# LSH attention and two MLP layers: products with v of the second batch four steps behind the scores, and the second layer's first w_in products ahead of the first layer's last w_out products

## Chip, cores and metric

One core of a Trainium2 chip. The metric is the device time of one execution in microseconds; the time before is a median of three runs. Engines: TensorE (PE; PEld is its weight load), VectorE (DVE), ScalarE (ACT), GpSimd (POOL), SyncE (SP, which here only issues transfers).

## What is computed

Attention in which a query sees only the keys of its own bucket (the signs of six projections), and then two MLP layers on the result, with sigmoid gates.

```python
# q, k, v: (2, 8, 768, 64); proj: (64, 6); w_in: (512, 2048); w_out: (2048, 512), two layers
mask = q_bucket[:, :, :, None] == k_bucket[:, :, None, :]
scores = np.where(mask, scale * np.matmul(q, k.transpose(0, 1, 3, 2)), -1000000000.0)
attn = np.exp(scores - np.max(scores, axis=-1, keepdims=True))
attn = attn / (np.sum(attn, axis=-1, keepdims=True) + 1e-09)
attn_out = np.matmul(attn, v)
x = attn_out.transpose(0, 2, 1, 3).reshape(B * S, H * D)      # 1536 x 512
h = x @ w_in;  g = h * (1.0 / (1.0 + np.exp(-1.702 * h)));  x = g @ w_out
h = x @ w_in2; g = h * (1.0 / (1.0 + np.exp(-h)));          return g @ w_out2
```

## The kernel before

**Precision.** Large operands are kept as a high and a low part, so that each layer product is three matmuls (`three` in `gemm2`, the inner loop of `gemm1`), and a product with v takes three per key block.

**Attention.** The 16 heads have six steps each, 96 steps in all; a step is 128 queries against 768 keys. `scores` (L408) makes four matmuls into the tile `pss`. `top` (L422) takes the row minimum on VectorE and copies the scores to `p`; `exps` and `p_high` run on ScalarE, `p_low` (L443) on GpSimd writes the low half into `hl`. Two steps share one `hl`: `p_turn` (L447) turns both on the odd step by one transposing transfer from SP's queue into `pt` (two buffers). `av` (L454) multiplies `pt` with v, 18 matmuls a step into `pav`, `norm` divides and turns the result into the MLP's tokens `XH`, `XL`. `ahead` prepares the next pair of heads on all engines; its `rows` (L355) copies bucket rows by four transfers on SP.

**Two batches.** The loop at L583 runs steps 0 to 47 and then 48 to 95. `LAG = 3` says how many steps later `av(j)` is written than the score step j's own turn. In the second batch `scores` has one buffer of `pss`, and between the steps the loop yields to the generator `mlp` of the first layer for token blocks 0 and 1 (`RATE` layer units a step).

**Layers.** `mlp` (L615) works in units of one to four slices of d_ff. For each unit and token block `gemm1` makes `psh` = x w_in and the gate (ScalarE L640, VectorE L641, ScalarE's cast to `gh` L642, GpSimd's `gl` L643), and `gemm2` makes `pso` = g w_out and adds it up in `part` (VectorE L675). `gemm2` of a unit and block is written behind `gemm1` of the next one; the last is written alone (L690). After the attention follow the first layer on blocks 2 and 3 (L762) and the second layer on all four (L765). Weights come as 64-bit words: `Weights.step` loads one piece (`raw`), makes fp32 of it by five operations (L173 ScalarE, L174 to L178 VectorE), then a high part (L180 ScalarE) and a low one (L181 GpSimd). One step is taken at each yield (`background`, L716).

**Order.** A scheduler sorts the instructions by priority into one queue for each engine, and each engine works its queue in order. `sooner` raises a task's priority by the offsets of `SOONER`: in the second batch `av` stands highest among the attention's tasks (400), `scores` has 200.

```python
            for i in range(first - lead, last + LAG + 1):
...
                at(av, i - LAG)
                at(top, i + lead - 1)
...
                at(p_turn, i - TUL)
                yield i
                if lead == 1:
                    at(scores, i + 1)
```

Of the kernel before, what the change touches and what calls it, by code (L numbers as in the profile page):

```python
# [21 lines left out]
def tile_lsh_attention_two_mlps(  # L22
# [15 lines left out]
    B, H, S, D = q.shape  # L38
# [23 lines left out]
    NBUF = 3  # L62
    LAG = 3
    TUL = 1
# [16 lines left out]
    RATE = (3.4, 2.85)  # L81
    SWITCH = HEADS // 2 * NC + LAG + 1
    RING = 3
# [168 lines left out]
    def attention(sp, s1, ps_m, ps_v, ahead_of, setup):  # L252
# [155 lines left out]
        def scores(j):  # L408
            n, c = steps[j]
            aq, ak = st["q", n], st["k", n]  # L410
            bq, bk = BQ[place(n)], BK[place(n)]
            ps = ahead_of["pool"].tile([P, 2, 512], F32, tag="s", name="pss")
            lq = aq.rearrange("p a b -> p (a b)")[:, c * P:(c + 1) * P]
            bq = bq[:, c * P:(c + 1) * P]
            for half in range(2):
                o = ps[:, half, 0:HS]
                T.matmul(o, lhsT=lq, rhs=ak[:, half, :], start=True, stop=False)  # L417
                T.matmul(o, lhsT=bq, rhs=bk[:, half * HS:(half + 1) * HS], start=False, stop=True)  # L418
            st["S", j] = ps[:, :, 0:HS]
# [34 lines left out]
        def av(j):  # L454
# [5 lines left out]
            o = st["av", g][:, c * (D + 1):(c + 1) * (D + 1)]  # L460
            for i in range(NC):
                hv, lv = vs[:, n % 2, i, 0:D + 1], vs[:, n % 2, i, D + 1:]
                T.matmul(o, lhsT=pt[:, i], rhs=hv, start=(i == 0), stop=False)  # L463
                T.matmul(o[:, 0:D], lhsT=pt[:, i], rhs=lv, start=False, stop=False)  # L464
                T.matmul(o, lhsT=pt[:, NC + i], rhs=hv, start=False, stop=(i == NC - 1))  # L465

# [115 lines left out]

        for lead, first, last in ((2, 0, N // 2), (1, N // 2, N)):  # L583
            def at(f, j):
# [30 lines left out]
    def mlp(layer, blocks, units, W, mp, ps_h, tanh, keep=()):  # L615
# [70 lines left out]
        for i, u in enumerate(seq):  # L686
            yield from gemm1(*u)
            if i != 1:
                yield from gemm2(*seq[max(i - 1, 0)])
        yield from gemm2(*seq[-1])  # L690

# [69 lines left out]
    ps_h = ctx.enter_context(tc.tile_pool(name="ps_h", bufs=8, space=PSUM))  # L761
    for _ in mlp(0, [2, 3], [first1] + cut, W, mp, ps_h, False):  # L762
        background()
    base = NF + len(again)
    for _ in mlp(1, [0, 1, 2, 3], [list(range(f, f + 4)) for f in range(base, base + NF, 4)], W, mp, ps_h, False):  # L765
        background()
# [30 lines left out]
```

## Time and profile before

| | |
|---|---|
| median of 3 runs | 806.49 us (803.45 to 806.79) |
| profiled execution, its own time | 809.91 us |
| its span | 807.9 us |
| PE busy | 740.4 us (92%) |
| DVE, ACT, POOL busy | 507.3, 422.4, 430.4 us |
| chain that ended last, by engine | PE 66%, DMA 13%, DVE 10%, issue 4%, ACT 3%, POOL 2% |

A busy PE counts modelled ends of pipelined matmuls. The first batch of the attention fills the span up to about 157 us, the second batch with the first layer's blocks 0 and 1 up to 394, the first layer's blocks 2 and 3 up to 530, and the second layer the rest.

### The profile page before, as it was taken

Reading aid. Unit: us, or ns where it says so; the run is one execution under the profiler, and the core shown is the slowest. Engines: PE = TensorE matmul, PEld = TensorE weight load, DVE = VectorE, ACT = ScalarE, POOL = GpSimd, SP = SyncE. Lnnn points to the kernel's source line nnn. Section 1 sums busy time; section 2 is a strip of 40 time slices with the busy share of each in tenths; the row PEclk is TensorE's granted clock in tenths of the full one; section 3 lists DMA queues with packets and bytes.
Section 4 is the critical chain, followed back from the end, with each engine's and each line's share of the span. In section 5 each row is a group of like instructions: output and inputs, shape, how many; then the busy total and the mean of one; then the engine's idle time right before and its main releaser. Section 6 shows DMA issues by size and latency. Waiting matters only on the chain.

```text
span 807.9 us, 14034 instructions
## 1 busy us (share of the span) xinstructions
PE 740.4 (92%) x5384; PEld 682.6 (84%) x5384; DVE 507.3 (63%) x932; ACT 422.4 (52%) x721; POOL 430.4 (53%) x345
## 2 busy tenths in 40 slices
PE   6786777678889999899999999979999999999998
PEld 5676666668878898899899999978998899989996
DVE  8987688967689798887332244999545744322222
ACT  6776576586778586676444134445545333311220
POOL 5675567877659666766633133567535334422220
PEclk9898888799999999999999999999999999999999
DMA  5999999999999998885597040333211300000112
GB/s 160 206 191 186 185 204 208 211 247 249 272 225 252 255 227 239 220 188 106 149 387 246 2 157 1 130 108 101 80 52 53 105 1 2 0 1 1 40 40 78
DMA packets 196270, 116.40 MB, mean 144 GB/s; under 512 B 153318, under 2 KB 175846, under 8 KB 196204
## 3 DMA queue, kind: packets, MB, share of 16 engines
q1 hardware_dynamic: 196044, 115.52, 57.5%
q8 instruction: 42, 0.69, 0.3%
q14 instruction: 24, 0.20, 0.1%
q10 hardware_dynamic: 160, 0.00, 0.0%
HBM read 56.63 MB, written 16.78 MB: 91 GB/s over the span
## 4 chain that ended last, share of the span: by engine, by line
PE 66%; DMA 13%; DVE 10%; issue 4%; ACT 3%; POOL 2%; SPq 0%; ACTq 0%; DVEq 0%; POOLq 0%
PE pso L666 29%; PE psh L632 28%; DMA pt<-hl 9%; PE pss L417 2%; PE psbit L345 2%; POOL hl L445 2%; DMA raw<-in_moe_w_in_dram 2%; DVE p L425 2%; PE pss L418 2%; DVE f L176 1%; ACT p L430 1%; PE pav L463 1%; PE pav L464 1%; PE pav L465 1%; DVE f L175 1%
## 5 line engine op out<-in xcount | busy, mean ns | idle before, releaser
L643 POOL TENSOR_TENSOR gl<-g,gh 128x384 fp32r<-128x384 f32 x128 | 136.0, 1064 | 195.7 <-ACT gh L642 183.6
L445 POOL TENSOR_TENSOR hl<-p,hl 128x768 f16<-128x768 f32 x96 | 162.6, 1700 | 71.9 <-ACT hl L441 37.4
L632 PE MATMUL psh<-XH,wih 128*128 128x384 f32 x512 | 174.2, 340 | 1.5 <-DVE part L675 1.0
L632 PE MATMUL psh<-XL,wih 128*128 128x384 f32 x512 | 172.9, 338 | 1.8 <-DVE XL L498 1.8
L632 PE MATMUL psh<-XH,wil 128*128 128x384 f32 x512 | 173.2, 338 | 0.0
L675 DVE SCALAR_TENSOR_TENSOR part<-pso,part 128x384 f32<-128x384 f32 (+1 forms) x124 | 72.6, 591 | 88.8 <-PE pso L666 88.6
L641 DVE TENSOR_TENSOR g<-g,psh 128x384 f32<-128x384 f32 x96 | 52.8, 551 | 117.5 <-ACT g L640 117.5
L430 ACT ACTIVATE p<-p,lo 128x768 f32<-128x768 f32 x96 | 89.7, 936 | 52.7 <-DVE p L425 52.2
L642 ACT CAST gh<-g 128x384 fp32r<-128x384 f32 x128 | 65.5, 513 | 78.7 <-DVE g L641 69.1
L425 DVE TENSOR_SCALAR_CACHE_REDUCE p<-pss 128x768 f32<-128x768 f32 x96 | 90.8, 948 | 15.3 <-PE pss L418 13.3
L632 PEld LDWEIGHTS psh<-XH,wih 128*128 128x128 f32 x512 | 97.5, 190 | 3.1 <-ACT XH L677 1.0
L632 PEld LDWEIGHTS psh<-XL,wih 128*128 128x128 f32 x512 | 97.6, 191 | 2.8 <-DVE XL L498 2.2
L632 PEld LDWEIGHTS psh<-XH,wil 128*128 128x128 f32 x512 | 97.3, 190 | 0.2 <-POOL wil L181 0.2
L640 ACT ACTIVATE g<-psh 128x384 f32<-128x384 f32 x96 | 46.8, 489 | 96.1 <-PE psh L632 95.2
L463 PE MATMUL pav<-VS,pt 128*128 128x65 f16 x576 | 64.4, 198 | 33.9 <-DMA pt<-hl 32.1
L666 PE MATMUL pso<-gh,woh 128*128 128x384 f32 x256 | 87.3, 347 | 6.5 <-ACT gh L642 4.3
L463 PEld LDWEIGHTS <-pt 128*128 128x128 f16 x576 | 54.6, 99 | 44.1 <-DMA pt<-hl 38.9
L666 PE MATMUL pso<-gh,wol 128*128 128x384 f32 x256 | 86.2, 337 | 0.0
L666 PE MATMUL pso<-gl,woh 128*128 128x384 f32 x256 | 86.1, 336 | 0.0
L417 PE MATMUL pss<-ak,aq 128*128 128x384 f32 x192 | 76.0, 397 | 10.8 <-DVE p L425 10.5
L666 PE MATMUL pso<-woh,gh 128*128 128x512 f32 x192 | 74.8, 390 | 0.2 <-ACT gh L642 0.2
L666 PE MATMUL pso<-wol,gh 128*128 128x512 f32 x192 | 75.0, 391 | 0.0
(119 smaller groups left out, 1572.0 us busy)
## 6 DMA issues: line engine op xcount, KB each, us to landing
raw<-in_moe_w_in_dram SPq DMA_DIRECT2D x32, 512.0 KB
raw<-in_moe_w_out_dram SPq DMA_DIRECT2D x32, 512.0 KB
spih<-wih SPq DMA_DIRECT2D x13, 256.0 KB
spil<-wil SPq DMA_DIRECT2D x13, 256.0 KB
spoh<-woh SPq DMA_DIRECT2D x13, 256.0 KB
spol<-wol SPq DMA_DIRECT2D x13, 256.0 KB
wih<-spih SPq DMA_DIRECT2D x13, 256.0 KB
wil<-spil SPq DMA_DIRECT2D x13, 256.0 KB
```

The lines of the kernel that those rows point to most:

```text
L417: T.matmul(o, lhsT=lq, rhs=ak[:, half, :], start=True, stop=False)
L425: V.tensor_scalar(p, st.pop(("S", j)), LOW, None, op0=ALU.min, op1=ALU.min, accum_out=lo)
L430: A.activation(p, p, AF.Exp, bias=lo, scale=-1.0)
L445: G.tensor_tensor(out=hl[:, 1], in0=st.pop(("p", j))[0], in1=hl[:, 0], op=ALU.subtract)
L463: T.matmul(o, lhsT=pt[:, i], rhs=hv, start=(i == 0), stop=False)
L632: T.matmul(h, lhsT=a[:, c], rhs=x[t][:, c], start=(n == 0), stop=(n == 3 * NDC - 1))
L640: A.activation(g, h, AF.Sigmoid, scale=beta)
L641: V.tensor_tensor(out=g, in0=g, in1=h, op=ALU.mult)
L642: A.copy(gh[:, f], g)
L643: G.tensor_tensor(out=gl[:, f], in0=g, in1=gh[:, f].bitcast(F32), op=ALU.subtract)
L666: T.matmul(y, lhsT=a, rhs=x, start=(n == 0), stop=(n == 3 * nf - 1))
L675: V.scalar_tensor_tensor(out=acc, in0=y, scalar=scale, in1=acc, op0=ALU.mult, op1=ALU.add)
```

## The change

`LAG` becomes a pair: three steps in the first batch, four in the second. In the second batch the products of step j are also tied behind the last score matmul of step j + 4 on TensorE (`issue_after`), so that the scheduler can't put them sooner; the last four steps, which have no such matmul, are free. `mlp` yields once more, "last", ahead of its last `gemm2`; at this place in the first layer's blocks 2 and 3 the caller takes four units of the second layer, its `gemm1` of the first four slices on block 0, each with a step of the weights.

```diff
-    LAG = 3
+    LAGS = (3, 4)
...
-    SWITCH = HEADS // 2 * NC + LAG + 1
+    SWITCH = HEADS // 2 * NC + LAGS[0] + 1
...
-                T.matmul(o, lhsT=bq, rhs=bk[:, half * HS:(half + 1) * HS], start=False, stop=True)
+                st["did", j] = T.matmul(o, lhsT=bq, rhs=bk[:, half * HS:(half + 1) * HS], start=False, stop=True).ins
...
-            for i in range(NC):
-                hv, lv = vs[:, n % 2, i, 0:D + 1], vs[:, n % 2, i, D + 1:]
-                T.matmul(o, lhsT=pt[:, i], rhs=hv, start=(i == 0), stop=False)
-                T.matmul(o[:, 0:D], lhsT=pt[:, i], rhs=lv, start=False, stop=False)
-                T.matmul(o, lhsT=pt[:, NC + i], rhs=hv, start=False, stop=(i == NC - 1))
+
+            first = st.get(("did", j + 4)) if j >= N // 2 else None
+            with tc.issue_after(first) if first is not None else nullcontext():
+                for i in range(NC):
+                    hv, lv = vs[:, n % 2, i, 0:D + 1], vs[:, n % 2, i, D + 1:]
+                    T.matmul(o, lhsT=pt[:, i], rhs=hv, start=(i == 0), stop=False)
+                    T.matmul(o[:, 0:D], lhsT=pt[:, i], rhs=lv, start=False, stop=False)
+                    T.matmul(o, lhsT=pt[:, NC + i], rhs=hv, start=False, stop=(i == NC - 1))
...
-        for lead, first, last in ((2, 0, N // 2), (1, N // 2, N)):
+        for lead, first, last, LAG in ((2, 0, N // 2, LAGS[0]), (1, N // 2, N, LAGS[1])):
...
                 yield from gemm2(*seq[max(i - 1, 0)])
+        yield "last"
         yield from gemm2(*seq[-1])
...
-    for _ in mlp(0, [2, 3], [first1] + cut, W, mp, ps_h, False):
+    base = NF + len(again)
+    second = mlp(1, [0, 1, 2, 3], [list(range(f, f + 4)) for f in range(base, base + NF, 4)], W, mp, ps_h, False)
+    for at_end in mlp(0, [2, 3], [first1] + cut, W, mp, ps_h, False):
         background()
-    base = NF + len(again)
-    for _ in mlp(1, [0, 1, 2, 3], [list(range(f, f + 4)) for f in range(base, base + NF, 4)], W, mp, ps_h, False):
+
+        if at_end == "last":
+            for _ in range(4):
+                next(second)
+                background()
+    for _ in second:
         background()
```

In the changed kernel the lines from `scores` on have numbers one to four higher. How it moves instructions, first in the second batch on TensorE, around the first product of step 78 (before: `pt_5266`, after the scores of step 81, `pss_5268`):

```order
L666 MATMUL pso_4004<-gh_3750,wol_3698 128x384
L417 MATMUL pss_5268<-ak_4192,aq_4271 128x384
L418 MATMUL pss_5268<-BK2_160,BQ2_156 128x384
...
L463 LDWEIGHTS pt_5266
L463 MATMUL pav_5273<-VS0_170,pt_5266 128x65
```

Now (`pt_5243` is steps 78 and 79, `pss_5245` and `pss_5286` are the scores of steps 81 and 82):

```order
L418 MATMUL pss_5245<-ak_4174,aq_4253 128x384
L419 MATMUL pss_5245<-BK2_160,BQ2_156 128x384
...
L467 MATMUL pav_5042<-VS0_170,pt_5157 128x65
...
L418 MATMUL pss_5286<-ak_4174,aq_4253 128x384
L419 MATMUL pss_5286<-BK2_160,BQ2_156 128x384
...
L636 MATMUL psh_3769<-XH1_64,wih_3492 128x384
...
L467 LDWEIGHTS pt_5243
L467 MATMUL pav_5291<-VS0_170,pt_5243 128x65
```

The products of step 78 stood right behind the scores of step 81. Now step 77's (`pt_5157`) stand there, and step 78's come behind the scores of step 82 and a unit of w_in.

On SP, the transfers between the transpositions of pairs 66 and 68 before (L186 stores parts of weights, L360 copies bucket rows):

```order
L451 DMA_TRANSPOSE pt_4465<-hl_4280 128x24x128
L186 DMA spih7_3148<-wih_3137 128x512
L292 DMA nv_4659<-in_v_dram 128x2x384
L360 DMA BK1_159<-mk_4448 13x768
L186 DMA spil7_3150<-wil_3138 128x512
L360 DMA BQ1_155<-mk_4448 13x768
L139 DMA raw_3411<-in_moe_w_out_dram 128x512
L360 DMA BK2_160<-mk_4448 13x768
L360 DMA BQ2_156<-mk_4448 13x768
L451 DMA_TRANSPOSE pt_4668<-hl_4462 128x24x128
```

Now those between pairs 68 and 70:

```order
L452 DMA_TRANSPOSE pt_4650<-hl_4439 128x24x128
L187 DMA spol6_3107<-wol_3095 128x512
L187 DMA spih7_3130<-wih_3119 128x512
L140 DMA raw_3355<-in_moe_w_in_dram 128x4x128
L361 DMA BK1_159<-mk_4425 13x768
L187 DMA spil7_3132<-wil_3120 128x512
L361 DMA BQ1_155<-mk_4425 13x768
L361 DMA BK2_160<-mk_4425 13x768
L361 DMA BQ2_156<-mk_4425 13x768
L452 DMA_TRANSPOSE pt_4825<-hl_4647 128x24x128
```

The four copies of bucket rows moved from ahead of pair 68's transposition to ahead of pair 70's; the next four stand ahead of pair 82's now, which before stood ahead of pair 78's.

At the change of layers, VectorE before (`g_7315` and `g_7333` are the third and fourth gate of the second layer's first unit, `f_...` are pieces of weights in conversion):

```order
L174 TENSOR_SCALAR f_7192<-f_7192 128x512
L175 TENSOR_SCALAR f_7192<-f_7192 128x512
L176 SCALAR_TENSOR_TENSOR f_7192<-raw_7131,f_7192 128x512
L641 TENSOR_TENSOR g_7315<-g_7315,psh_7302 128x384
L178 SCALAR_TENSOR_TENSOR f_7192<-raw_7131,f_7192 128x512
L174 TENSOR_SCALAR f_7211<-f_7211 128x512
L175 TENSOR_SCALAR f_7211<-f_7211 128x512
L176 SCALAR_TENSOR_TENSOR f_7211<-raw_7150,f_7211 128x512
L641 TENSOR_TENSOR g_7333<-g_7333,psh_7320 128x384
```

Now (`g_7275` and `g_7293` are the third and fourth gate, `part_6150` to `part_6186` the first layer's last sums):

```order
L175 TENSOR_SCALAR f_7192<-f_7192 128x512
L679 SCALAR_TENSOR_TENSOR part_6150<-pso_7298,part_6150 128x384
L176 TENSOR_SCALAR f_7192<-f_7192 128x512
L679 SCALAR_TENSOR_TENSOR part_6162<-pso_7305,part_6162 128x384
L645 TENSOR_TENSOR g_7275<-g_7275,psh_7262 128x384
L679 SCALAR_TENSOR_TENSOR part_6174<-pso_7312,part_6174 128x384
L177 SCALAR_TENSOR_TENSOR f_7192<-raw_7131,f_7192 128x512
L679 SCALAR_TENSOR_TENSOR part_6186<-pso_7319,part_6186 128x384
L645 TENSOR_TENSOR g_7293<-g_7293,psh_7280 128x384
L179 SCALAR_TENSOR_TENSOR f_7192<-raw_7131,f_7192 128x512
```

The fourth gate stands ahead of the last operation of `f_7192` and of all of the next piece's, which before stood ahead of it. The order of VectorE up to the end of the first layer's last gate is the same in both.

## Rows read from the trace of the kernel before

**Rows 1.** Stretches: length, busy PE, PEld, DVE, ACT, POOL (instructions), PE clock, DMA share, GB/s

```profile
156.60:394.00 237.40, 218.61 (x2028) 202.62 (x2027) 186.15 (x364) 168.50 (x276) 164.42 (x128) 0.99 0.95 220
394.00:530.50 136.50, 135.73 (x783) 135.08 (x781) 63.76 (x108) 50.98 (x99) 52.48 (x47) 1.00 0.46 158
530.50:562.00 31.50, 26.99 (x133) 25.12 (x134) 29.75 (x39) 15.68 (x31) 24.39 (x20) 0.95 0.26 87
```

**Rows 2.** TensorE's waits from 180 to 394 us: total, times, longest

```profile
PE pav L463 <- DMA pt<-hl: 9.4, 8, 2.3
```

**Rows 3.** Timeline, pair 78: score, low part, transposition, product; [idle before <-releaser]

```profile
310.64 0.34 PE L417 MATMUL pss<-ak,aq 128*128 128x384 f32 x1
...
314.51 1.65 POOL L445 TENSOR_TENSOR hl<-p,hl 128x768 f16<-128x768 f32 x1
...
318.38 5.32 SPq L451 DMA_TRANSPOSE pt<-hl  x1
...
325.38 0.20 PE L463 MATMUL pav<-VS,pt 128*128 128x65 f16 x1 [2.29 <-DMA pt<-hl]
```

**Rows 4.** Timeline, first products of pairs 54, 56, 68; pair 74's transposition

```profile
197.04 0.20 PE L463 MATMUL pav<-VS,pt 128*128 128x65 f16 x1 [1.81 <-DMA pt<-hl]
...
208.34 0.20 PE L463 MATMUL pav<-VS,pt 128*128 128x65 f16 x1 [1.51 <-DMA pt<-hl]
...
271.69 0.20 PE L463 MATMUL pav<-VS,pt 128*128 128x65 f16 x1 [1.78 <-DMA pt<-hl]
...
293.41 4.56 SPq L451 DMA_TRANSPOSE pt<-hl  x1
```

**Rows 5.** Busy time by stretches: the two stretches at half clock

```profile
272.70:276.10 3.40, 3.40 (x12) 3.40 (x11) 1.86 (x3) 2.29 (x3) 2.18 (x3) 0.50 1.00 351
535.60:538.90 3.30, 3.30 (x12) 3.30 (x12) 3.30 (x6) 2.36 (x5) 3.30 (x4) 0.50 0.23 91
```

**Rows 6.** The chain that ended last: start us, us, what

```profile
199.62 8.66 DMA pt<-hl
...
208.54 0.03 PE pav L464
...
265.48 6.17 DMA pt<-hl
...
482.62 8.32 PE psh L632 x48
...
589.06 8.20 PE pso L666 x36
```

**Rows 7.** Timeline, pair 68: low part on GpSimd, last row copy and transposition on SP

```profile
259.18 1.66 POOL L445 TENSOR_TENSOR hl<-p,hl 128x768 f16<-128x768 f32 x1
...
264.60 0.76 SPq L360 DMA_DIRECT2D BQ<-mk  x1
265.48 4.16 SPq L451 DMA_TRANSPOSE pt<-hl  x1
```

**Rows 8.** Timeline, TensorE at the change of layers

```profile
534.80 0.44 PE L666 MATMUL pso<-gh,woh 128*128 128x384 f32 x1 [4.33 <-ACT gh L642]
...
556.54 0.50 PE L666 MATMUL pso<-woh,gh 128*128 128x512 f32 x1 [0.21 <-ACT gh L642]
...
559.88 0.33 PE L632 MATMUL psh<-XH,wih 128*128 128x384 f32 x1
```

**Rows 9.** Timeline, GpSimd and VectorE at the change of layers

```profile
514.29 1.48 POOL L181 TENSOR_TENSOR wil<-f,wih 128x512 fp32r<-128x512 f32 x1 [1.29 <-ACT wih L180]
...
530.49 0.78 DVE L174 TENSOR_SCALAR f<-f 128x512 f32<-128x512 f32 x1 [1.83 <-ACT f L173]
...
533.60 0.55 DVE L641 TENSOR_TENSOR g<-g,psh 128x384 f32<-128x384 f32 x1
...
550.42 1.04 DVE L178 SCALAR_TENSOR_TENSOR f<-raw,f 128x512 int32<-128x512 int32 x1
...
555.40 0.54 DVE L641 TENSOR_TENSOR g<-g,psh 128x384 f32<-128x384 f32 x1
```

## The prediction, made before the change was run

> **What bounds the kernel now.** I read the view by stretches first. From 156.6 to 394 us, where the second batch's attention runs mixed with the first layer's products, TensorE is busy 218.61 of 237.40 us, and no other engine passes 186.15; from 394 to 530.5 it is busy 135.73 of 136.50, and in the 31.5 us around the change of layers 26.99 [rows 1]; behind that the long runs of matmuls follow each other again [rows 6]. So the end is set by TensorE's work and its gaps, and a step that is moved on TensorE is worth the gap that it closes, no more. Second came the list of TensorE's waits after 180 us: products with v that wait for a turned tile, 9.4 us in 8 waits, stand far ahead of the rest [rows 2]. Third, one of these waits followed back through the engines. I number the score steps from 0; the second batch is 48 to 95, and two steps share one transposition, so "pair 78" is steps 78 and 79. The scores of step 79 begin at 310.64, GpSimd ends its low part at 314.51 + 1.65 = 316.16, the transposition is issued at 318.38, and the product of step 78 starts at 325.38 after 2.29 us of idle [rows 3]: 14.7 us from score to product, of which 7.0 belong to the transposition. The other large waits are 1.81 (pair 54), 1.51 (pair 56) and 1.78 us (pair 68) [rows 4]; four small ones make up the missing 2.0. [...] Half a clock for 3.4 us loses 1.7 us, for 3.3 us 1.65.
>
> **The products, four steps behind.** Nothing is added or removed on TensorE: 384 score matmuls, 1,728 products and all layer products stay, so the cost is in the order alone. What counts is how much TensorE work stands between the first score matmul of a pair's second step and the pair's first product. I counted it in the two orders at 0.173 us for a matmul of 384 columns (48 in 8.32) and 0.03 for a product [rows 6]. Before, the products of the two steps stood together; now each follows the scores four steps on, alone. Seven of the eight waiting pairs get more work in between: pair 68 from 14.4 to 21.8 us, pair 78 from 11.9 to 16.4, pairs 62, 66 and 84 one to two us more, pair 92 half a us, pair 54 from 12.9 to 13.6. I take away 1.78 and 2.29 for pairs 68 and 78, the 2.0 of the small four, and 0.7 of pair 54's 1.81: 6.7 us. Against it, two pairs lose cover. Pair 56 goes from 10.4 to 8.5, which lengthens its wait by 1.9; pair 74 from 13.1 to 11.4, and though it has no wait of note now, its transposition was issued only at 293.41 [rows 4] and takes at least 6.17 us like the others [rows 6], so that it landed hardly ahead of its product; I charge 1.5. The net of this is 6.7 - 3.4 = 3.3 us.
>
> The transpositions share SP's queue with every other transfer, and a moved step takes its transfers along. Before, four copies of bucket rows stand ahead of the transposition of pair 68. GpSimd had finished that pair at 259.18 + 1.66 = 260.84, but SP, still issuing (the last copy at 264.60 for 0.76), reached the transposition at 265.48: 4.64 us late [rows 7]. In the changed order four such copies stand right ahead of pairs 70 and 82. Pair 70's distance grows by 4.1 us, which takes up most of such a delay; pair 82's does not grow. I charge 2 us for both together, between nothing and 2 x 4 us, since how long SP stands behind depends on when the issues ahead become ready. With pair 68's wait the stretch of half clock behind it should go too: 1.7 us back. Sum for the attention: 3.3 - 2 + 1.7 = 3.0 us gained. Its ends are all waits and the half clock, 9.4 + 1.7 = 11.1 us gained, and 6.7 - 3.4 - 8 = 4.7 us lost.
>
> [...] The rows have 6.17 and 8.66 us from issue to landing [rows 6], and SP alone is held 4.16 and 5.32 us by the issue [rows 3, 7]. [...]
>
> **The products of the second layer, put ahead.** At the change of layers TensorE stands idle 4.33 us up to 534.80 for the gate of the last single unit, then runs at half clock [rows 8, 5]. The wait is long because VectorE, busy 29.75 of these 31.5 us [rows 1], has conversions of weights ahead of that gate: it starts it at 533.60 [rows 9]. The change puts 48 matmuls of the second layer, 8.3 us at full clock, into that hole. Their inputs are there: the tokens of block 0 are old, and the last of their four weight pieces was finished at 514.29 + 1.48 [rows 9]. So the 4.33 us, the later 0.21 and the 1.65 of half clock, 6.2 us in all, would be the gain if TensorE alone counted. It does not. The second layer's first w_out products need the gates of those 48, and these gates stand on VectorE behind the same conversions. From 530.49 to the fourth gate at 555.40 VectorE has next to no pause. In the changed order that gate has one conversion less ahead of it, which is the stretch from 550.42 to 555.40, 4.98 us [rows 9]. It then starts at about 550.4; its product followed 556.54 - 555.40 = 1.14 us later [rows 8, 9], so at 551.6. Behind it stand 9 + 3 matmuls of 512 columns at 8.20 / 36 = 0.228 [rows 6] and 12 of 384, 2.7 + 2.1 us, up to the unit that before starts at 559.88 [rows 8]: 556.4. The gain is 3.5 us, between 0 (VectorE held by something that does not move) and 6.2. TensorE will wait at these gates instead of the old place; that is what is late next.
>
> The layer work that the shift pushes out of the attention, about 66 matmuls or 11.4 us, runs behind the last product and costs the same there, since TensorE has no gap to fill there. The added yield costs no instruction.
>
> **Sum.** 3.0 + 3.5 = 6.5 us. The profiled execution took 809.91 us, so it would become 803.4; against the median of the three runs, 806.49, I forecast 800.0. About 0.5%, 4 us, is what a measurement of this kernel can tell from no change.
>
> **Rivals.**
> 1. All of it goes: no pair waits any more, no half clock, and VectorE is not what the gates wait for. 806.5 - 11.1 - 6.2 = 789; with a part of it left, 789 to 795. For it speaks that seven of eight pairs get more cover; against it, pairs 56 and 74.
> 2. The waits only change places. TensorE's order becomes tighter by what is saved, so the same 14 us from score to product reach further into the work, and what pair 68 and 78 gain pairs 56, 70, 74 and 82 lose; the change of layers gives 1 to 2 us. 803 to 808. The chain through VectorE, ScalarE, GpSimd and SP is left as it was, which speaks for it.
> [...]
> 4. Slower: SP's queue decides. If pairs 70 and 82 are both late by the full 4.64 us, and, as SP is held for 4 to 6 us by each transposition, each passes half of it to the next pair, that is 9.3 + 4.6 = 13.9 us of new waits. Less 3.3 and 3.5 it leaves 7 us more: 813. It decides from about 7 us of new lateness on. Against it: their products are now later as well, and pair 70's cover has grown.
>
> **How the numbers follow.** Forecast 0.45 (796 to 802), rival 1 0.12, rival 2 0.28, rival 3 0.03, rival 4 0.12. Forecast and rival 1 are faster by over 0.5%: 0.57. Rivals 2 and 3 lie within 0.5%: 0.31. Rival 4 is slower: 0.12. The range from 791 to 810 takes in most of rival 1 and all of rivals 2 and 3; some of rival 4 and the best end are left out. The bounds of the unknown costs would reach from 806.5 - 17.3 = 789 to 806.5 + 4.7 = 811.
>
> **What would show it.** Right: in the stretch of the second batch the products' waits for the turned tile fall from 9.4 to 6 to 8 us, with pair 56's wait over 3 us and none at pairs 68 and 78; no half clock near 272 us. At the change of layers no idle time of 4 us, but two to four waits of 0.4 to 1.3 us at the second layer's first w_out products, released by ScalarE's copy of the gate, and some 3.5 us less up to the same unit. Wrong: waits of over 2 us at pairs 70 and 82 behind row copies on SP (rival 4), the products' waits below 2 us (rival 1), or an idle VectorE while TensorE waits for gates, which would mean that my bound there is not the one.

## The result, and the profile after

The changed kernel is slower: 813.92 us (median of 10 runs, 811.13 to 817.49) against 806.64 for the kernel before on the same chip (10 runs, 803.45 to 810.45), a ratio of 1.0082 with a 95% interval of 1.0059 to 1.0105. The forecast was 800.0, in a range of 791 to 810. The profiled execution took 817.49 us with a span of 815.7 (before: 809.91 and 807.9). Profiled executions of the kernels below lie up to 4.3 us from the median of their kernel (these two 3.3 and 3.6 us above it), so trace and ratio are always read together.

What decides is seen only when the second batch's attention is cut out exactly, from its first score matmul (step 48) to its last product (step 95). Before, by stretches (length, busy time of PE, PEld, DVE, ACT, POOL with instruction counts, mean granted PE clock, DMA share, GB/s): all instructions, then those of the first layer's w_in products (psh), then of its w_out products (pso):

```profile
151.50:393.80 242.30, 223.51 (x2042) 207.36 (x2043) 190.11 (x370) 172.03 (x280) 169.37 (x130) 0.98 0.95 221
151.50:393.80 242.30, 75.89 (x384) 68.86 (x384) 17.52 (x32) 15.43 (x32) 0.98 0.95 221
151.50:393.80 242.30, 74.36 (x361) 62.19 (x362) 28.32 (x52) 3.79 (x8) 0.98 0.95 221
```

In the changed kernel, in the same view and order, they are:

```profile
151.20:388.70 237.50, 216.92 (x1976) 197.01 (x1977) 183.80 (x361) 166.53 (x271) 163.09 (x124) 0.97 0.97 225
151.20:388.70 237.50, 71.84 (x360) 64.12 (x360) 16.40 (x30) 14.41 (x30) 0.97 0.97 225
151.20:388.70 237.50, 66.56 (x319) 54.46 (x320) 24.64 (x45) 3.84 (x8) 0.97 0.97 225
```

First-layer matmuls in the stretch: 384 + 361 = 745 before, 360 + 319 = 679 now. The 66 that left are worth 66 x 0.173 = 11.4 us [rows 6] and run behind the last product. But the stretch became only 242.3 - 237.5 = 4.8 us shorter. So 11.4 - 4.8 = 6.6 us were lost there, of the 7.8 by which the span grew. From the end of the stretch on the span has 815.7 - 388.7 = 427.0 us and had 807.9 - 393.8 = 414.1, 12.9 more: there the 11.4 us of work cost their full time. I call **stretch less layer work** the length minus 0.173 us for each first-layer matmul in it: 242.3 - 128.9 = 113.4 us before, 237.5 - 117.5 = 120.0 now. Up to the start of the stretch the two agree (151.5 and 151.2).

How much of this is chance shows from repeats. Two of the experiments below, e1 and e3, have in this stretch the instructions of the kernel before, on every engine in the same order:

```profile
151.30:390.40 239.10, 222.28 (x2042) 206.42 (x2043) 190.03 (x370) 171.85 (x280) 169.66 (x130) 0.99 0.95 223
150.30:392.80 242.50, 226.81 (x2042) 210.79 (x2043) 190.23 (x370) 171.54 (x280) 169.20 (x130) 0.96 0.95 220
```

So one order took 242.3, 239.1 and 242.5 us. The order of the changed kernel took 237.5, and 239.3 in e2. A single trace is good to some 3 us; by the means, 241.3 and 238.4, the stretch became 2.9 us shorter and 8.5 us were lost in it.

TensorE's waits of the changed kernel from 180 to 394 us (total, times, longest):

```profile
PE pav L467 <- DMA pt<-hl: 8.7, 6, 2.9
PE pss L418 <- DVE p L426: 1.9, 2, 1.2
PE pss L419 <- DMA BQ<-mk: 1.7, 2, 1.2
PE pav L467 <- DVE xn L483: 1.1, 1, 1.1
PE pso L670 <- DVE g L642: 0.9, 1, 0.9
```

Against [rows 2] the products wait nearly as long (9.4 before), in fewer places, and 3.6 us of waits of score matmuls stand beside them (0.3 before), behind VectorE's reading of the score before (L426) and behind the bucket rows' copies (BQ<-mk). The timeline has the largest (start, length, instruction, idle before it and releaser):

```profile
207.04 0.20 PE L467 MATMUL pav<-VS,pt 128*128 128x65 f16 x1 [2.88 <-DMA pt<-hl]
...
242.01 0.20 PE L467 MATMUL pav<-VS,pt 128*128 128x65 f16 x1 [1.35 <-DMA pt<-hl]
...
271.90 0.45 PE L418 MATMUL pss<-ak,aq 128*128 128x384 f32 x1 [1.23 <-DVE p L426]
...
327.93 0.42 PE L419 MATMUL pss<-BK,BQ 128*128 128x384 f32 x1 [1.21 <-DMA BQ<-mk]
...
353.03 0.20 PE L467 MATMUL pav<-VS,pt 128*128 128x65 f16 x1 [1.42 <-DMA pt<-hl]
...
387.41 0.20 PE L467 MATMUL pav<-VS,pt 128*128 128x65 f16 x1 [2.25 <-DMA pt<-hl]
```

They are pairs 56 and 64, a score behind VectorE, a score behind a row copy, and pairs 86 and 94. Pairs 64, 86 and 94 had no wait before; pairs 68 and 78 have none now. The granted clock, by stretches:

```profile
173.50:176.90 3.40, 3.40 (x33) 3.05 (x32) 0.97 (x3) 3.38 (x7) 2.01 (x3) 0.51 0.96 276
207.70:211.10 3.40, 3.40 (x26) 3.09 (x24) 1.47 (x3) 1.38 (x2) 1.03 (x1) 0.50 1.01 310
388.60:392.00 3.40, 3.40 (x14) 3.40 (x12) 1.31 (x4) 0.00 (x0) 0.00 (x0) 0.50 0.00 0
552.50:559.20 6.70, 5.94 (x14) 4.68 (x15) 5.60 (x9) 4.48 (x10) 6.48 (x6) 0.50 0.23 78
```

The two half-clock stretches of [rows 5] are gone; three of the same length came up in or right behind the attention, two of them within 1.2 us of the ends of the waits at 207.04 and 387.41, and one of twice the length at the change of layers, whose timeline is:

```profile
550.32 0.50 PE L670 MATMUL pso<-woh,gh 128*128 128x512 f32 x1 [1.15 <-ACT gh L646]
550.58 0.54 DVE L645 TENSOR_TENSOR g<-g,psh 128x384 f32<-128x384 f32 x1
551.16 0.51 ACT L646 CAST gh<-g 128x384 fp32r<-128x384 f32 x1 [0.89 <-DVE g L645]
551.76 2.41 POOL L647 TENSOR_TENSOR gl<-g,gh 128x384 fp32r<-128x384 f32 x2
...
553.26 0.79 PE L670 MATMUL pso<-woh,gl 128*128 128x512 f32 x1 [1.34 <-POOL gl L647]
```

The idle time of 4.33 us [rows 8] is gone. In its place the second layer's first w_out products wait for the third gate's copy (1.15) and then for the low part that GpSimd makes (1.34), and run at half clock.

### The profile page after: what moved, and what is told of

The parts are those of the page before. It is cut to its first block, busy times and chain, and to the rows that moved or that the text cites. A ratio compares the mean times of both kernels' runs of the same rounds, so it can differ in the third digit from the quotient of the medians.

```text
span 815.7 us, 14040 instructions
## 1 busy us (share of the span) xinstructions
PE 748.7 (92%) x5384; PEld 685.3 (84%) x5384; DVE 504.9 (62%) x932; ACT 421.5 (52%) x721; POOL 429.5 (53%) x345
## 4 chain that ended last, share of the span: by engine, by line
PE 61%; DMA 14%; DVE 10%; ACT 6%; issue 5%; POOL 3%; SPq 1%; ACTq 0%; DVEq 0%; POOLq 0%
PE pso L670 28%; PE psh L636 26%; DMA pt<-hl 7%; DMA raw<-in_moe_w_in_dram 2%; DVE p L426 2%; ACT p L431 2%; POOL hl L446 2%; DMA raw<-in_moe_w_out_dram 2%; PE pss L418 2%; PE pss L419 1%; DMA nv<-in_v_dram 1%; ACT hl L442 1%; PE pav L467 1%; PE psbit L346 1%; DVE f L177 1%
## 5 line engine op out<-in xcount | busy, mean ns | idle before, releaser
L426 DVE TENSOR_SCALAR_CACHE_REDUCE p<-pss 128x768 f32<-128x768 f32 x96 | 90.6, 946 | 16.9 <-PE pss L419 14.9
L644 ACT ACTIVATE g<-psh 128x384 f32<-128x384 f32 x96 | 46.8, 489 | 98.0 <-PE psh L636 97.3
L467 PE MATMUL pav<-VS,pt 128*128 128x65 f16 x576 | 67.3, 200 | 32.6 <-DMA pt<-hl 29.6
L670 PE MATMUL pso<-gh,woh 128*128 128x384 f32 x256 | 89.2, 352 | 1.6 <-DVE g L642 1.0
L670 PE MATMUL pso<-woh,gl 128*128 128x512 f32 x192 | 75.8, 398 | 1.3 <-POOL gl L647 1.3
```

What stands on the lines that cost most here:

```text
L426: V.tensor_scalar(p, st.pop(("S", j)), LOW, None, op0=ALU.min, op1=ALU.min, accum_out=lo)
L644: A.activation(g, h, AF.Sigmoid, scale=beta)
L670: T.matmul(y, lhsT=a, rhs=x, start=(n == 0), stop=(n == 3 * nf - 1))
```

## The experiments

There are 18 kernels in five sets, each set beside runs of the kernel before on its chip. In the table, "products" says how many steps behind the scores the products with v are written, and "tied" that they also have to stand behind a score matmul, as in the change. "Clock" is the mean granted clock in the stretch, and "less work" the stretch less layer work, both of the profiled execution, cut and counted as above.

| run | products | ratio (95%) | stretch us | clock | layer matmuls | less work us |
|---|---|---|---|---|---|---|
| before | 3 behind | 1 | 242.3 | 0.98 | 745 | 113.4 |
| changed | 4, tied | 1.0082 (1.0059 to 1.0105) | 237.5 | 0.97 | 679 | 120.0 |
| e1 | 3 | 0.9995 (0.9977 to 1.0012) | 239.1 | 0.99 | 745 | 110.2 |
| e2 | 4, tied | 1.0127 (1.0104 to 1.0150) | 239.3 | 0.95 | 679 | 121.8 |
| e3 | 3 | 0.9946 (0.9928 to 0.9964) | 242.5 | 0.96 | 745 | 113.6 |
| e4 | 4, tied by pairs | 1.0080 (1.0053 to 1.0108) | 242.0 | 0.96 | 709 | 119.3 |
| f1 | 3 | 1.0141 (1.0113 to 1.0170) | 234.8 | 0.95 | 661 | 120.4 |
| f2 | 4, tied, paced | 1.0063 (1.0042 to 1.0084) | 244.8 | 0.97 | 757 | 113.8 |
| f3 | 4 | 1.0069 (1.0041 to 1.0097) | 235.5 | 0.97 | 679 | 118.0 |
| f4 | 3, paced | 1.0220 (1.0191 to 1.0248) | 259.2 | 0.96 | 768 | 126.3 |
| g1 | 3, paced | 1.0063 (1.0040 to 1.0085) | 244.2 | 0.97 | 751 | 114.3 |
| g2 | 3 | 1.0047 (1.0026 to 1.0069) | 250.1 | 0.98 | 763 | 118.1 |
| g3 | 4, paced | 1.0109 (1.0083 to 1.0136) | 250.6 | 0.95 | 757 | 119.6 |
| h1 | 4, tied, 3 holds | 1.0029 (1.0009 to 1.0048) | 244.7 | 0.99 | 751 | 114.8 |
| h2 | 3, 6 holds | 1.0055 (1.0033 to 1.0077) | 245.8 | 0.98 | 768 | 112.9 |
| h3 | 4, 1 hold | 1.0078 (1.0047 to 1.0109) | 246.5 | 0.98 | 745 | 117.6 |
| h4 | 4, tied, 3 holds | 0.9980 (0.9961 to 0.9999) | 242.5 | 0.98 | 751 | 112.6 |
| d1 | 4, tied | 1.0027 (1.0004 to 1.0049) | 238.4 | 0.98 | 721 | 113.7 |
| d2 | 3 | 1.0090 (1.0063 to 1.0117) | 247.6 | 0.98 | 763 | 115.6 |
| d3 | 3 | 1.0073 (1.0047 to 1.0099) | 242.7 | 0.97 | 727 | 116.9 |

The change of layers is as in the kernel before in e2, e4, f1 to f3, g1, g3, h1 to h3, d2 and d3; as in the changed kernel in e1 and d1; with more cover (as in e3) in e3, f4, g2 and h4.

### The two parts apart: e1, e2

e1 has the change of layers alone:

```diff
-    LAGS = (3, 4)
+    LAGS = (3, 3)
...
-            first = st.get(("did", j + 4)) if j >= N // 2 else None
+            first = None
```

> The change with its attention part undone: lag 3 in both batches and no tie behind a score matmul; only the second layer's first four units stand ahead of the first layer's last w_out products. By the theory that the loss sits in the second batch's attention (its TensorE gaps grew from about 34 to 42 us in the two traces, those around the change of layers only from 6.9 to 7.4), this is 0 to 1 us beside the kernel before: 806 to 808 us, ratio 0.999 to 1.002. By the rival that the layer part costs the time (its half-clock stretch grew from 3.4 to 6.8 us and it shifts the weights' steps), it is 5 to 8 us slower, ratio 1.006 to 1.010. By my prediction's step for this part it would be 3.5 us faster, ratio 0.996.

e2 has the delay of the products alone:

```diff
-        if at_end == "last":
-            for _ in range(4):
-                next(second)
-                background()
```

> The change with its layer part undone: products with v of the second batch four steps behind and tied behind the scores, layers in the old order (a yield more, that issues nothing). By the theory that the attention holds the loss: 6 to 8 us slower than before, ratio 1.007 to 1.010, with the products' waits for turned tiles near 9 us as before, score waits (for the minimum on VectorE and for row copies) of 4 us or more after 180 us, and three stretches of half clock between 157 and 394 us. By the rival: within 1 us of before.

The layers alone make no difference, and the delay alone is 1.3% slower. The changed kernel, with both, is 0.8% slower, as if the layers gained 3.6 us beside the delay. But e2 and the changed kernel have the same order up to the end of the stretch, and over all their executions the mean granted clock was 0.962 in e2 and 0.967 in the changed kernel, which is up to 0.005 x 816 = 4 us; so that gain may be the clock's alone. The kernel before had 0.967 to 0.969 in the five sets, so the clock of its executions doesn't explain why the changed kernel is slower.

In e1 TensorE and VectorE work like this at the change of layers:

```profile
538.65 0.50 PE L670 MATMUL pso<-woh,gh 128*128 128x512 f32 x1 [1.16 <-ACT gh L646]
538.92 0.54 DVE L645 TENSOR_TENSOR g<-g,psh 128x384 f32<-128x384 f32 x1
...
541.61 0.50 PE L670 MATMUL pso<-woh,gl 128*128 128x512 f32 x1 [1.36 <-POOL gl L647]
...
568.70 0.49 PE L670 MATMUL pso<-woh,gh 128*128 128x512 f32 x1 [0.29 <-ACT gh L646]
...
570.22 0.50 PE L670 MATMUL pso<-woh,gl 128*128 128x512 f32 x1 [0.79 <-POOL gl L647]
```

The gates hold TensorE as in the changed kernel, and a second time 30 us on, where the kernel before has no wait.

### More cover, and ties by pairs: e3, e4

e3 is e1 with the second layer's w_in products of the second token block ahead of its first w_out products too, so that the gates have 48 matmuls more (8.3 us) to come in:

```diff
-            if i != 1:
+            if i != 1 - layer:
```

> The layer part alone, and in the second layer the first w_out products stand behind the w_in products of the second token block, where before they stood right behind those of the first one: 8.3 us more of TensorE work between the gates' inputs and their use. If the gates behind VectorE's conversions are what TensorE still waits for at the change of layers, the 2.6 us of waits and the half clock behind them go: 6 to 7 us faster than before, ratio 0.991 to 0.993, no half clock between 530 and 570. If the wait follows the products to their new place (VectorE late by more than 8.3 us), it is 0 to 2 us faster.

e4 is e2 with both products of a pair tied to one score:

```diff
-            first = st.get(("did", j + 4)) if j >= N // 2 else None
+            first = st.get(("did", j - j % 2 + 4)) if j >= N // 2 else None
```

> The attention part alone, with the products of both steps of a pair tied behind the scores of the first step plus four, so that they stay together as before. If the single products crowd the score steps (one score tile in PSUM, its minimum not yet taken), most of the score waits go and this is 2 to 5 us faster than the attention part as changed, ratio 1.002 to 1.006. If the loss comes from the later row copies on SP and from pairs that lose cover, it is the same as that within 1.5 us.

e3 is faster than the kernel before by 0.54% (803.19 us). Its waits at the change of layers are short:

```profile
540.52 0.44 PE L636 MATMUL psh<-XH,wih 128*128 128x384 f32 x1 [0.66 <-DVE g L645]
...
545.77 0.44 PE L636 MATMUL psh<-XH,wih 128*128 128x384 f32 x1 [0.79 <-DVE part L679]
...
553.80 0.50 PE L670 MATMUL pso<-woh,gl 128*128 128x512 f32 x1 [0.83 <-POOL gl L647]
```

e4 changed with the tie how much work was pushed out (709 stayed), and lost less than e2.

### Is it the work pushed out? f1 to f4

The next four ask whether the loss is the work that left the stretch. f1 is the kernel before, products three behind and no tie; only the scores' place in the scheduler's order is made more urgent, which pushes out 84 matmuls:

```diff
-    ... {'scores': 200, 'evict': 50, 'norm': 300, ...
+    ... {'scores': 400, 'evict': 50, 'norm': 300, ...
```

> The kernel before, lag 3 and no tie, with one number changed: the scores' priority in the second batch from 200 to 400. The scheduler then puts 660 of the first layer's matmuls between the first score of step 48 and the last product, where before has 744 and the changed kernel 678. Theory: the stretch of the second batch takes 238 to 243 us whatever stands in it, because its chain through the other engines sets its length, and each layer matmul that is left out of it costs its 0.173 us behind it; then this is 84 x 0.173 = 14.5 us of work moved out, 10 to 16 us slower than before, ratio 1.012 to 1.020. Rival: lag and tie themselves cost the time (lost cover, crowded scores); then lag 3 with fewer layer matmuls is within 3 us of before.

f2 is e2 with the work put back: the first score matmul of step j is "paced", that is issued behind the n-th first-layer matmul, n = 14.5 (j - 51). `fill` is the list of these matmuls in program order.

```diff
+            due = min(int(14.5 * (j - 51)), len(fill))
             for half in range(2):
                 o = ps[:, half, 0:HS]
-                T.matmul(o, lhsT=lq, rhs=ak[:, half, :], start=True, stop=False)
+                with tc.issue_after(fill[due - 1]) if due > 0 and half == 0 else nullcontext():
+                    T.matmul(o, lhsT=lq, rhs=ak[:, half, :], start=True, stop=False)
```

> The attention part of the change alone (lag 4 and tie), with each step's scores also tied behind a number of the first layer's matmuls (14.5 a step), so that 756 of them stand in the stretch where the attention part alone has 678. Theory of the constant stretch: 78 x 0.173 = 13.5 us of work are back in it, so it is 8 to 14 us faster than the attention part alone and 0 to 4 us faster than before, ratio 0.995 to 1.000, with the stretch still 237 to 245 us long. Rival, lag and tie cost by themselves: the stretch gets longer by what is put back, and the time stays 6 to 10 us above before.

f3 is e2 without the tie:

```diff
-            first = st.get(("did", j + 4)) if j >= N // 2 else None
+            first = None
```

> The attention part alone with lag 4 but without the tie behind the score matmuls: the products are written a step later and the scheduler is free. It puts 678 layer matmuls in the stretch, like the tied one. Theory of the constant stretch: as slow as the tied one, 8 to 12 us above before, ratio 1.010 to 1.015. If the tie itself were the cost (products forced behind scores), it is within 4 us of before.

f4 is e3 with f2's pacing at 17.0 a step:

> Lag 3, the layer part with the second layer's first w_out products behind its second w_in products, and the pacing with 17 layer matmuls a step: all 768 of the first layer's matmuls for blocks 0 and 1 stand in the stretch, 24 more than before. Theory of the constant stretch: 24 x 0.173 = 4.2 us less than the same without pacing, which was 0.9946 of before: ratio 0.988 to 0.992, 797 to 801 us. If the stretch has come to TensorE's own bound with so much in it, or the even pacing makes scores late, it is 0 to 4 us slower than without pacing, ratio 0.995 to 1.000.

f1 shows a loss without any delay: 84 matmuls (14.5 us) left, the stretch got 7.5 us shorter, the ratio is 1.0141. Its mean granted clock over all executions, 0.965, is near that of the kernel before (0.967); but the place of its scores changed too. f2 is better than e2 and still slower than before. f3 has the 679 matmuls of e2 and of the changed kernel and is at 1.0069, where they are at 1.0127 and 1.0082: the number pushed out doesn't set the time alone. f4 is the worst of all: with 768 matmuls in the stretch, paced evenly, it is 259.2 us long. The number alone isn't the reason there either, since h2 below has 768 in 245.8 us. So a stretch with less work in it is not short by as much, and more work in it is not free.

### Pacing, more work, no tie: g1 to g3

g1 is the kernel before with f2's pacing at 15.7 a step, g3 is f3 with it at 12, and g2 is e3 with a faster planner:

```diff
-    RATE = (3.4, 2.85)
+    RATE = (3.8, 3.2)
```

> The kernel before (products three steps behind, no tie), with the same pacing of the first layer's matmuls as in f2, at 15.7 a step, which places 749 of them in the second batch's stretch, about as many as f2's 756 and the 744 of before. Theory (what counts is the layer work placed in the stretch, and beside it the lag and the tie lengthen the stretch by some 5 us): without lag and tie the time is that of before, 806 to 808 us, and f2's 5 us are the lag's and the tie's. Rival (pacing by itself costs the 5 us, by holding score matmuls back, and lag and tie are neutral once the fill is the same): 811 to 813 us, with new waits at the score matmuls.

> e3 with the planner's rate raised from (3.4, 2.85) to (3.8, 3.2), nothing else: 761 first-layer matmuls in the second batch's stretch in place of 743, 18 more or 3.1 us by 0.173 us each. Theory (layer work placed in the stretch is partly free, since TensorE is not its bound): 1 to 3 us below e3, that is a ratio of 0.990 to 0.994 to the kernel before. Rival (the stretch is full at 744 matmuls, as f4 with its 768 in strict pacing suggested): the stretch grows by at least 3.1 us and the time is that of e3, 0.9946, or above.

> Products four steps behind without the tie to the scores (as f3), with pacing of the first layer's matmuls at 12 a step, which places 755 of them in the second batch's stretch, as f2 has with the tie (756) and g1 with lag three (749). Theory (the stretch costs nothing extra by the lag alone once its fill is that of before): 806 to 809 us, and against f2 it is 4 to 5 us faster, which is then the tie's cost. Rival (the lag itself costs, by products that pile up at places with less cover): 811 to 813 us as f2 and f3, with waits of products for turned tiles of 14 us or more.

g1 is as slow as f2: holding a score at nearly every step costs 5 us by itself, so f2 does not tell what the delay costs. g2's theory fails: 18 matmuls more than e3 (3.1 us) lengthen the stretch by 7.6 us. So does g3's, at 1.0109.

### Holds at a few steps: h1 to h4

h1 is e2 with f2's construction at three steps alone, called holds; h4 is h1 with e3's change of layers:

```diff
-            due = min(int(14.5 * (j - 51)), len(fill))
+            due = {60: 107, 72: 305, 84: 533}.get(j, 0)
```

h2 has it in the kernel before with `{60: 107, 66: 206, 72: 305, 78: 419, 84: 533, 90: 638}`, h3 in f3 with `{84: 533}`.

> e2 (products four steps behind and tied to the scores, second layer as before) with three holds only: the first score matmul of steps 60, 72 and 84 stands behind the 107th, 305th and 533rd first-layer matmul, the counts that the kernel before has at these steps. By this 737 of them are placed in the second batch's stretch (744 before, 678 in e2). Theory (the loss is the work pushed behind the stretch): 59 matmuls or 10.2 us come back into the stretch, most of it free, so 806 to 810 us, that is a ratio of 0.998 to 1.004 and at least 8 us below e2. Rival (the delay of the products and its tie cost by themselves): 813 to 818 us, as e2.

> Control for h1: products three steps behind as before, no tie, with holds at six steps at the counts of the kernel before, 737 first-layer matmuls in the stretch. Theory (a few holds cost next to nothing): 806 to 809 us, ratio 0.999 to 1.003. Rival (any hold costs, as the pacing at every step did in g1): 811 to 813 us; then h1 is to be held against this run and not against the kernel before.

> Products four steps behind without the tie, with one hold at step 84 (behind the 533rd first-layer matmul), 737 of them in the stretch. Theory (work pushed out is the loss): 805 to 809 us, 4 to 8 us below f3, which has 678 of them. Rival (the delay itself): 813 us as f3.

> h1 with the second layer's first products ahead and its second unit's w_in products ahead of its first w_out products, as in e3; 749 first-layer matmuls in the stretch. Theory (the two parts add, and with the work back in the stretch the delay is neutral): e3's gain of 4.4 us against h1, so 802 to 806 us, ratio 0.994 to 0.999. Rival (the delay costs by itself): 809 us or more.

The count in the first three of these expectations, 737, was wrong: the traces have 751, 768 and 745. h1, with the delay and the tie of e2 and 72 matmuls more, by stretches as above:

```profile
153.70:398.40 244.70, 224.63 (x2048) 206.81 (x2049) 189.06 (x371) 172.00 (x281) 171.02 (x131) 0.99 0.97 219
```

e2, the same:

```profile
150.00:389.30 239.30, 219.85 (x1976) 201.38 (x1977) 182.65 (x361) 166.48 (x271) 163.08 (x124) 0.95 0.97 223
```

72 x 0.173 = 12.5 us came back and lengthened the stretch by 5.4; the ratio fell from 1.0127 to 1.0029, as the theory wanted. But the pair has a rival that no run sets aside: e2's stretch had a granted clock of 0.95 and h1's 0.99, and 0.04 x 240 = 9.6 us is more than the 7.1 in question. Over all executions the clocks are 0.962 and 0.968, up to 5 of the 9 us between the two medians. h1's waits from 180 to 394 us:

```profile
PE pso L673 <- ACT part L680: 3.6, 3, 1.6
PE pso L673 <- DVE g L645: 3.2, 4, 1.4
PE pav L470 <- DMA pt<-hl: 2.6, 4, 1.0
```

Here the delay does what it says, 2.6 us of waits for turned tiles in place of 9.4 [rows 2]. But the first layer's w_out products now wait 6.8 us, and nothing is gained. h4 adds e3's gain to it, about as expected, and does not reach e3. h3's theory fails: 66 matmuls (11.4 us) more than f3 lengthened its stretch by 11.0 us, and it stays at 1.0078. h2 is no clean control, with 23 matmuls more than before. It came out at 1.0055, as its rival said and above h1, so what holds cost by themselves isn't known, nor what the delay is worth in h1 without them.

### Are the DMA engines the floor? d1 to d3

The stretch moves the same bytes in both kernels, with the DMA engines nearly always busy (share 0.95 before, 0.97 now). The DMA view of it before:

```profile
DMA packets 102465, 53.49 MB, mean 221 GB/s; under 512 B 85065, under 2 KB 93513, under 8 KB 102440
```

And of the changed kernel:

```profile
DMA packets 102507, 53.50 MB, mean 225 GB/s; under 512 B 85108, under 2 KB 93556, under 8 KB 102482
```

d1 (the changed kernel) and d2 (the one before) write only half of each weight tile that is spilled, that is copied out to DRAM for a second pass, and read that half twice:

```diff
...
-                    d = spill.tile([P, NDC, P], F32, name=f"sp{kind}{part}{block[1]}")
-                    SP.dma_start(out=d, in_=t.bitcast(F32))
+                    d = spill.tile([P, 2, P], F32, name=f"sp{kind}{part}{block[1]}")
+                    SP.dma_start(out=d, in_=t[:, 0:2].bitcast(F32))
```

and d3 is the kernel before with some spills written twice (11 in the trace, 2.9 MB, where 13 were expected):

```diff
+                    if kind == "o" and part == "h" and stage[0] == 1:
+                        twice = spill.tile([P, NDC, P], F32, name=f"tw{block[1]}")
+                        SP.dma_start(out=twice, in_=t.bitcast(F32))
```

> The changed kernel, with half of each spilled weight tile left out: the copies to DRAM (51 of 256 KB in the second batch's stretch) write the first half alone, and the later reload reads that half twice, so that part of the first layer's second pass is computed with wrong weights. The number of transfers in the stretch and all other instructions stay; 6.5 of 53.5 MB go, and the scheduler's order then holds 719 first-layer matmuls in the stretch (678 in the changed kernel, 7.1 us more). Theory (the DMA engines, 0.97 busy, are the stretch's floor): by bytes the floor falls from about 230 to 202 us, TensorE bounds instead, the stretch less the layer work in it falls from 120.0 to 113 us or below, and the time to 800 to 808 us. Rival (latency from score to product, or TensorE's order): the stretch less the layer work stays at 118 to 121, the time at 812 to 816 us.

> The kernel before with the same halved spills (part of the first layer's second pass with wrong weights); 761 first-layer matmuls in the stretch (744 before). Theory (DMA engines are the floor, at 0.95 nearly so in the kernel before): stretch less layer work falls from 113.4 by 3 to 8 us, the time to 798 to 804 us. Rival: no change beyond 0.5%, 803 to 810 us.

> The kernel before with 13 more copies of 256 KB to DRAM in the stretch (each high part of a w_out tile is written to a second place that nothing reads), 3.3 MB on 53.5 or 6.2%; 725 first-layer matmuls in the stretch (744 before). The 13 issues take about 13 x 0.45 = 6 us of SP's queue. Theory (DMA engines are the floor): 230 us of busy DMA engines become 244, the stretch less the layer work grows by 8 to 14 us, and the time to 814 to 822 us. Rival: the stretch less the layer work grows by no more than 3 us, the time is 806 to 811 us.

d2 by stretches:

```profile
154.30:401.90 247.60, 226.82 (x2060) 211.19 (x2061) 191.18 (x373) 173.35 (x283) 173.11 (x133) 0.98 0.83 189
```

The DMA share fell to 0.83 and the bytes by 6.7 MB, yet the stretch grew and the kernel became 0.9% slower. So the DMA engines are not the floor in the kernel before. d1 alone came out near the DMA theory, with 113.7 us less work where its rival said 118 to 121; but 42 matmuls came into its stretch too, 7.3 us, which by e2 and h1 would give most of the 4.4 us that it gained. d3 lost 5.9 us, and the 18 matmuls that left its stretch explain 18 x 0.173 = 3.1 of them at most. So the added transfers cost something too, and where isn't shown.

## Why the prediction was wrong

**The step that failed** is the one on the pushed-out work: "about 66 matmuls or 11.4 us, runs behind the last product and costs the same there, since TensorE has no gap to fill there". The number was right, 66, and so was the cost behind. What failed is "the same": it took for granted that the stretch gives back the 11.4 us, and it gave back 4.8 (2.9 by the means of the repeats). TensorE had 242.3 - 223.5 = 18.8 us without a matmul in the stretch before, and 237.5 - 216.9 = 20.6 now, 1.8 more. The other 4.8 us are busy time, which fell by 6.6 only: the same 972 products with v are busy 44.0 us and were 39.0, by stretches before and now:

```profile
151.50:393.80 242.30, 38.96 (x972) 7.88 (x24) 0.98 0.95 221
151.20:388.70 237.50, 43.96 (x972) 7.90 (x24) 0.97 0.97 225
```

On TensorE's queue they stand in 76 pieces now and stood in 52. A piece is a run of them without another matmul in between. This is where the time shows, and no full account: busy times hold modelled ends of matmuls, so part of the 5.0 us can be the view's, and f3 has 39.4 us and 48 pieces and loses as well.

Over 19 of the 20 kernels of the table (f4 left out) a straight line through stretch against matmuls has a slope of 0.11 us for each, with 2.4 us of scatter, where each costs 0.173 behind the stretch. By that line 66 matmuls out lose 66 x 0.06 = 4 us; by the pair e2 and h1, (12.5 - 5.4) / 72 = 0.1 us each, they lose 6.5. The rest of the 6.6 us, 0 to 2.6, is within the scatter, which is no wider than that of one order in its repeats. f3 and h3 are the pair that this doesn't fit. Nor is it shown that the missing work itself is the cause: the emptier stretches also had the lower clocks on the whole, and if stretch x (1 - clock) is taken off each one first, the slope becomes 0.16 and 66 matmuls lose 1 us. Whether the missing work brought the half clock, no run tells; one order alone had 0.98, 0.99 and 0.96 (before, e1, e3). For the changed kernel itself the clock explains little: by its trace 237.5 x 0.03 - 242.3 x 0.02 = 2 us of the 6.6, by all its executions about nothing. The line's upper end is open too: from 745 on, more work has not paid (g2, h2, d2, f4), of which g2 alone has neither holds nor other transfers. The kernel before may sit near a turning point.

**The products four steps behind** were priced at 3.3 us gained. Pairs 68 and 78 lost their waits and pair 56 got 2.88 (1.51 + 1.9 = 3.4 had been worked out). But pairs 64, 86 and 94, which the sum had at nothing, wait 1.35 + 1.42 + 2.25 = 5.0 us, and the scores wait too: 9.4 became 8.7 for the products (8.8 in e2), not 6 to 8, and all rows of that view together are 15.3 us, and were 12.6. The sum had taken the time from score to product as fixed for each pair and counted only the work put in between; for pair 94 that time was at most 12.1 us and is 13.4. The 9.4 us were one execution's, too: in e1 and e3, with the same order, they are 8.9 and 7.3. This is rival 2's mechanism, the waits change places, at a worse time than its 803 to 808. How long a transposition takes with other transfers beside it (DMA share 0.95 in the stretch) is shown by the chain of the kernel before: two of 768 KB took 6.17 and 8.66 us [rows 6], and an ordinary load of 512 KB took 6.42:

```profile
215.30 6.42 DMA raw<-in_moe_w_in_dram
```

With the work of the kernel before in the stretch the delay hasn't been shown to gain anything: h1, 1.0029, holds included.

**SP's row copies** were charged 2 us, as late transpositions at pairs 70 and 82. Neither pair waits. The copies' own readers do, 1.7 us. That the size came out near is luck, since the place was wrong; rival 4 did not happen, though its time, 813, was the one that came.

**The half clock** of 272.7 us went, as expected. Its 1.7 us were an estimate, half of the 3.4 us at a granted clock of 0.50 [rows 5]. The timeline before has eleven matmuls of 384 columns from one start to the other:

```profile
272.65 0.48 PE L666 MATMUL pso<-gh,wol 128*128 128x384 f32 x1
...
276.12 0.34 PE L632 MATMUL psh<-XL,wih 128*128 128x384 f32 x1
```

They take 3.47 us, where 11 x 0.173 = 1.90 us [rows 6], so 1.6 us more. Three other such stretches came, up to 3 x 1.7 = 5.1 us in this trace. But the term was no property of the order. In e1, with the order of the kernel before, pair 68's product waits too, 1.54 us up to 270.64, and no half clock follows:

```profile
270.00:275.00 5.00, 4.36 (x47) 4.21 (x48) 3.15 (x7) 2.96 (x5) 3.68 (x3) 1.00 0.96 282
```

Over all executions the mean granted clock of the two kernels is the same within 0.002.

**The change of layers**, 3.5 us forecast between 0 and 6.2, is worth nothing that can be told from no change: e1, 0.9995, that is 0.4 us with an interval from 1.0 us lost to 1.9 gained. The bound was right, VectorE's gates; the fourth starts at 550.58, 0.26 us behind the third gate's product. What was left out is what follows the gate: ScalarE's copy, then GpSimd's low part, 2.41 us for two, for which the products waited 1.34 us; in the changed kernel half a clock for 6.7 us, up to 3.4 us; in e1 the next gates, 30 us on. That more cover helps is shown by e3: 803.19 us, 4.3 us below e1, with the same order up to there.

**Open** stays what sets the length of the stretch. It is not TensorE's work alone (f1, e2) and not the DMA bytes (d2). It could be the chain from one score to the next through VectorE, ScalarE and GpSimd, to which the scores' waits in the changed kernel point; no run tests that. How much of the loss is the half clock, and whether emptier stretches bring it, is open as well. Why f3's order with its work put back (g3, h3) stays slow wasn't found.

## What to carry to other kernels

When a scheduler mixes two kinds of work in one stretch, compare ahead of the run how much of the second kind each order holds there: here work that was pushed out cost its full time behind and gave back only part of it in front (4.8 of 11.4 us), though TensorE was 92% busy there. Profile one order more than once before reading a few microseconds out of it: the same stretch came out 3.4 us apart. A wait that is moved away by a longer distance need not be a gain: in h1 the products' waits fell to 2.6 us, and others of 6.8 us came in their place. Work put ahead to cover a wait must also cover what is made out of the awaited result (here a copy and a low part, which TensorE awaited 1.15 and 1.34 us in place of the 4.33), or the wait comes back one place later.

## What was not expected of the hardware

The same two waits at the change of layers, 1.15 and 1.34 us in the changed kernel and 1.16 and 1.36 in e1, were followed by half a clock for 6.7 us in the one and by none in the other: e1 by stretches, over its two waits,

```profile
538.60:545.00 6.40, 4.79 (x17) 3.06 (x18) 5.15 (x8) 3.25 (x7) 6.40 (x5) 1.00 0.26 83
```

So whether idle time of a given length is followed by a half clock can't be read off its length alone. And in the kernel before a DMA share of 0.95 with 53.5 MB looked like a bound and was none: at 0.83 and 46.8 MB (d2) the stretch was no shorter.
